# Batches 0 and 1 as a pair with seven block products for eight, in a fused attention and MLP kernel

## The chip, the cores and the metric

The kernel runs on one core of a Trainium2 chip. The metric is device time in microseconds, the median over executions of the same program. A core has five engines that work side by side, each through its own instructions in order: TensorE (PE in the profile, with its weight loads as PEld), VectorE (DVE), ScalarE (ACT), GpSimd (POOL) and SyncE (SP, which here only issues DMAs). Semaphores order them among each other.

## The reference

Attention with 16 query heads on 4 key and value heads, then an MLP block on its output:

```python
def _attn_ref(q, k, v):               # q (8,16,384,64), k and v (8,4,384,64)
    ...
    scores = scale * np.matmul(q, k.transpose(0, 1, 3, 2))
    ...                               # softmax
    return np.matmul(attn, v)

def _moe_ref(x, alpha1, beta1, w_tok, alpha2, beta2, w_ch1, w_ch2, lam):
    a1 = alpha1 * x + beta1           # x (8,384,1024): the heads side by side
    tok = np.einsum('ts,bsd->btd', w_tok, a1)
    u = x + lam * tok
    a2 = alpha2 * u + beta2
    ch = np.maximum(a2 @ w_ch1, 0.0) @ w_ch2      # 1024 -> 4096 -> 1024
    return u + lam * ch
```

Most of the arithmetic is in the two large products, with W1 (`w_ch1`) and W2 (`w_ch2`).

## The kernel before

Matmuls take bf16 operands and sum in fp32 PSUM banks. One batch is 384 tokens. Weights come from HBM in fp32 and are cast by DMAs that POOL issues (`load_w1`: 512 KB in bf16 per chunk of 256 columns, into a ring of six slots; `load_w2`, quarters and rows of W2).

**Batches 0 and 1** are worked singly. `side(0)` is batch 0's attention, written out as a list of steps: `k_transpose` and `q_transpose` (turned on PE), `scores(i)` (18 pieces; each ends with an exp on ACT into one of six places in `hT`), `av(p)` for a pair of heads (product with v, then reciprocal and scaling on DVE), `a1(p)` (times alpha1 on DVE), `tok(p)` (token product with the transposed `w_tok`, which `wtok_transpose` turns; the beta row comes as one more matmul of `R` and `H`; then u on DVE), and `a2_transpose(p)`, which for batch 0 turns u on PE (L357) and scales it with alpha2 on ACT. `main(b)` then makes all of the first product (`h`: 256 matmuls of 384 columns, L532, for batch 0 partly L223) and all of the second (`ch`: 192 of 512 columns, L570) for the one batch. Batch 1's attention stands among main(0)'s matmuls, that of batches 2 and 3 among main(1)'s. The table `plan` says at which step of which stage each piece of work is recorded.

**The later batches** go in pairs, `pair(i)`: with two batches as two block rows, each product is made of seven block products instead of eight. In the first product (`X`, `Y`, `Z`, L723) a slice g covers two column tiles e of each half of W1: seven products o of four matmuls for each e. The left sides come from `opb(k)`, made by `sums_a` on DVE; the right ones are W1 blocks or their differences (`sum_w1`, four on DVE per slice). In the second product (`C`, L789) seven products of three row tiles and 16 matmuls each run over `hid`, with W2's blocks and their combinations, which `sum_w2` made once on DVE and put into seven scratch tensors `w2s` in HBM, from where `fetch` reads them for every pair. The next two batches' attentions are recorded among the second product's matmuls, their k and q turned by DMA (`flip_k`, `flip_q`, issued by SP), a2 made on DVE and turned by DMA (`a2_transpose`) or for a few pieces on PE (`turn`). `spill` writes u to the output; the product's result is added to it by an accumulating DMA (`store`), scaled by lam on DVE (`scaled`).

The order on each engine is the order of recording in the source (`tc.manual_schedule`): nothing is moved by a scheduler. The alpha2, beta1 and lam rows reach all partitions by way of `load_row_set` (four copies of half a row by an SP DMA) and `to_all` (a shuffle on DVE). POOL issues its DMAs on eight semaphores in turn, so that one waits for the eighth before it.

Of the kernel before, what the change touches and what calls it, by code (L numbers as in the profile page):

```python
# [12 lines left out]
def kernel(  # L13
# [21 lines left out]
    nc = tc.nc  # L35
# [10 lines left out]
    G = Hq // Hkv  # L46
# [9 lines left out]
    NPL = 2  # L56
# [14 lines left out]
    threes, pairs = [], {}  # L71
# [5 lines left out]
    w2 = arena.rearrange("p (t h d) -> p t h d", t=NH, h=2)  # L77
    hid = arena.rearrange("p (t e) -> p t e", t=NH)[:, :, :5 * S].rearrange("p t (k s) -> p t k s", k=5)
    w1 = const.tile([P, RING, NDT, CW * P], bf, tag="w1", name="w1")
# [5 lines left out]
    BE = NDT // 2 * S  # L85
    ops = const.tile([P, 7 * BE], bf, tag="ops", name="ops")
    a2Ts = [ops[:, :NDT * (S + 16)].rearrange("p (a s) -> p a s", a=NDT),
            ops[:, 5 * BE:].rearrange("p (a s) -> p a s", a=NDT)]

    def opb(k):  # L90
        return ops[:, k * BE:(k + 1) * BE].rearrange("p (a s) -> p a s", a=NDT // 2)
# [26 lines left out]
    def row(nt):  # L118
        return nt % NH, nt // NH
# [21 lines left out]
    def load_k(b, hs=(0, 2)):  # L141
        if b > 1:
            k_tile(b)
            for a in range(2):
                nc.gpsimd.dma_start(out=k2s[b][:, :, a], in_=by_head(k[b]))
            return
        for h in hs:
            ks[b, h // 2] = t = hTf[:, 7680 + 384 * h:8448 + 384 * h].bitcast(f32).rearrange(
                "p (h st d) -> p h st d", h=2, st=NST)
            nc.sync.dma_start(out=t, in_=by_head(k[b, h:h + 2]))  # L150

    def place_k(b, i, hs=(0, 1)):
        if b not in k2s:
            k_tile(b)
        copies = [nc.gpsimd.tensor_copy] * 2
        if b == 1 or b == 0 == i:
            copies = (nc.vector.tensor_copy, nc.vector.tensor_copy if i else nc.scalar.copy)
        lo, hi = hs[0], hs[-1] + 1
        for a in range(2):
            copies[a](out=k2s[b][:, 2 * i + lo:2 * i + hi, a], in_=ks[b, i][:, lo:hi])  # L160
# [26 lines left out]
    def load_w2(dw, r, h):  # L187
        cs = slice(dw * 512, (dw + 1) * 512)
        nc.gpsimd.dma_start(out=w2[:, 4 * r:4 * r + 4, h, cs], in_=w2src[:, h * NH + 4 * r:h * NH + 4 * r + 4, cs])

# [5 lines left out]
    def three():  # L196
        if pairs:
# [11 lines left out]

    def evac(eng):  # L210
        return nc.scalar.copy if eng == "ACT" else nc.vector.tensor_copy


    early = {}
    FIRST = (0, 1, NH, NH + 1)
# [844 lines left out]
```

## Time and profile before

| what | us |
| --- | --- |
| median of 3 timed runs (739.28 to 741.14) | 739.38 |
| span of the profiled execution, first to last instruction | 737.7 |
| PE busy in it | 731.3 |
| DVE busy | 515.4 |
| ACT busy | 325.2 |
| POOL busy, its DMA issues with it | 164.0 |
| start of the first product's unbroken part (L532) | 36.3 |
| first matmul of the second product of batch 0 (L570) | 74.9 |
| first matmul of the pair's first product (L723) | 242.1 |

The profiled execution has no time of its own beside its span; the median of the timed ones is 1.65 us above the span. Busy times count each instruction from its start to its end, and pipelined matmuls overlap, so that the distance from one start to the next is the price of one. Each timeline line gives start, length, engine, source line, operation, output and input, shapes and count; a line of the stretches gives span, and for each engine busy time and instructions, then the granted TensorE clock, the DMA share and GB/s. The page's GB/s row has 40 equal slices of the span.

### The profile page before, as it was taken

What the parts mean: (1) busy time and instruction counts of PE and PEld (TensorE: products, weight loads), DVE (VectorE), ACT (ScalarE), POOL (GpSimd) and SP (SyncE); (2) the same over time, 40 slices, a digit from 0 to 9 for tenths busy, and PEclk for the clock granted to TensorE, in tenths of its full rate; (3) what the DMA queues carried; (4) which work ended last, traced back from release to release, by engine and by line L of the source; (5) the groups of instructions that cost most, each with busy time, mean ns of one, the idle gap of its engine ahead of it and who ended that gap; (6) DMA issues with size and microseconds to landing.
All of it is one profiled execution on the core that took longest, in us unless ns stands there. A gap on an engine that the chain in (4) does not pass through costs nothing.

```text
span 737.7 us, 14512 instructions
## 1 busy us (share of the span) xinstructions
PE 731.3 (99%) x5769; PEld 418.9 (57%) x5769; DVE 515.4 (70%) x993; ACT 325.2 (44%) x469; POOL 164.0 (22%) x211
## 2 busy tenths in 40 slices
PE   8999999999999999999999999999999999999998
PEld 5866555566555566655555566555555566654444
DVE  7773366457587889749777987847968988762354
ACT  7632431455332566653334366664343266660000
POOL 9434221420000232211012244020002222000011
PEclk9999999999999999999999999999999999999999
DMA  9999999999999999999979999998989999937965
GB/s 187 194 201 200 207 216 174 176 187 208 217 271 257 179 221 212 260 269 201 296 186 219 181 145 192 207 246 199 269 242 152 223 136 143 173 115 262 288 189 103
DMA packets 218017, 151.32 MB, mean 205 GB/s; under 512 B 88660, under 2 KB 197060, under 8 KB 217948
## 3 DMA queue, kind: packets, MB, share of 16 engines
q0 software_dynamic: 120304, 64.60, 67.0%
q1 hardware_dynamic: 96956, 85.33, 42.7%
q8 instruction: 45, 0.74, 0.4%
q10 hardware_dynamic: 688, 0.46, 0.2%
q14 instruction: 24, 0.20, 0.1%
HBM read 154.84 MB, written 38.27 MB: 262 GB/s over the span
## 4 chain that ended last, share of the span: by engine, by line
PE 93%; DVE 3%; DMA 3%; SPq 1%; issue 0%; ACT 0%; DVEq 0%
PE C L789 30%; PE X L723 17%; PE h L532 10%; PE ch L570 9%; PE Y L723 8%; PE sc L279 4%; PE Z L723 4%; PE sc L315 4%; PE sc L340 3%; DMA ops<-a 2%; PE h L223 1%; DMA hT<-in_moe_lam_dram 1%; PE tok L340 1%; SPq L176 0%; PE av L315 0%; DVE xr L323 0%
## 5 line engine op out<-in xcount | busy, mean ns | idle before, releaser
L288 ACT ACTIVATE es<-sc 128x1024 bf16<-128x1024 f32 x126 | 121.4, 1023 | 155.9 <-PE sc L279 144.8
L789 PE MATMUL C<-w,arena 128*128 128x512 bf16 (+2 forms) x744 | 168.3, 372 | 0.0
L789 PEld LDWEIGHTS <-arena 128*128 128x128 bf16 x1040 | 94.8, 98 | 100.5 <-issue 5.1
L728 ACT ACTIVATE hT<-X,bias 128x384 f32<-128x384 f32 x144 | 83.7, 582 | 61.8 <-PE X L723 54.8
L723 PEld LDWEIGHTS <-w 128*128 128x128 bf16 x768 | 75.1, 98 | 50.1 <-issue 0.2
L517 POOL DMA_DIRECT2D out_dram<-hT x33 | 28.8, 871 | 283.5 <-DVE hT L688 106.1
L570 PE MATMUL ch<-arena,hT 128*128 128x512 bf16 x384 | 90.8, 379 | 0.0
L185 POOL DMA_DIRECT2D w<-in_moe_w_ch_dram x68 | 62.8, 965 | 98.2 <-PE X L723 34.2
L532 PE MATMUL h<-ops,w 128*128 128x384 bf16 (+1 forms) x480 | 83.3, 327 | 0.3
L723 PEld LDWEIGHTS <-pad 128*128 128x128 bf16 x576 | 56.4, 98 | 37.2
L723 PE MATMUL X<-ops,w 128*128 128x384 bf16 x384 | 70.2, 326 | 0.0
L723 PE MATMUL X<-ops,pad 128*128 128x384 bf16 x384 | 70.2, 326 | 0.0
L789 PE MATMUL C<-pad,arena 128*128 128x512 bf16 (+2 forms) x296 | 70.2, 373 | 0.0
L532 PEld LDWEIGHTS <-w 128*128 128x128 bf16 x480 | 45.4, 98 | 29.8 <-issue 2.1
L570 PEld LDWEIGHTS <-hT 128*128 128x128 bf16 x384 | 34.7, 98 | 36.8 <-issue 2.5
L347 DVE TENSOR_TENSOR xr<-sc,xr 128x384 f32<-128x384 f32 x56 | 31.0, 553 | 24.3 <-PE sc L340 24.3
L315 PEld LDWEIGHTS <-es 128*128 128x128 bf16 x1008 | 38.3, 97 | 12.4
L340 PEld LDWEIGHTS <-wtokT 128*128 128x128 bf16 x576 | 37.5, 98 | 11.8 <-DVE a L330 0.8
L279 PE MATMUL sc<-qT,kT 64*128 64x384 bf16 (+2 forms) x576 | 41.8, 271 | 0.7 <-DVE xr L323 0.3
L320 DVE RECIPROCAL rinv<-sc 128x6 f32<-128x6 f32 x56 | 10.8, 192 | 44.3 <-PE sc L315 44.1
L315 PE MATMUL sc<-v,es 128*128 128x65 bf16 x1008 | 39.9, 193 | 0.0
L723 PE MATMUL Z<-ops,w 128*128 128x384 bf16 x192 | 39.0, 326 | 0.0
(138 smaller groups left out, 910.3 us busy)
## 6 DMA issues: line engine op xcount, KB each, us to landing
w<-in_moe_w_ch_dram POOLq DMA_DIRECT2D x68, 512.0 KB, 10.7
w<-w2s SPq DMA_DIRECT2D x60, 512.0 KB, 4.6
pad<-w2s SPq DMA_DIRECT2D x24, 512.0 KB, 7.2
out_dram<-xr SPq DMA_DIRECT2D x56, 192.0 KB, 6.1
out_dram<-hT POOLq DMA_DIRECT2D x33, 256.0 KB, 6.0
arena<-in_moe_w_ch_dram POOLq DMA_DIRECT2D x16, 512.0 KB, 20.0
w2s<-arena SPq DMA_DIRECT2D x28, 256.0 KB, 4.9
q_raw<-in_q_dram POOLq DMA_DIRECT2D x28, 192.0 KB, 10.6
```

The lines of the kernel that those rows point to most:

```text
L185: nc.gpsimd.dma_start(out=w1[:, w1_slots[c]], in_=w1src[:, :, c * CW * P:(c + 1) * CW * P])
L279: nc.tensor.matmul(out=sc[:, hh, k % 4:k % 4 + n], lhsT=kT[r, 2 * p // G, BLK[hh][sk], :], rhs=qT[r, p, st:st + n, :], start=True, stop=True)
L288: nc.scalar.activation(out=e, in_=sc, func=EXP, scale=scale_qk)
L315: nc.tensor.matmul(out=av[:, hh, sq, :], lhsT=ess[k // 4][:, m % 2, k % 4, :], rhs=vb[:, sk, hk, :], start=(sk == 0), stop=(sk == NST - 1))
L340: nc.tensor.matmul(out=ps[:, tt, :], lhsT=wtokT[:, st, tt * P:(tt + 1) * P], rhs=a1s[p][:, st, :], start=(st == 0), stop=(st == NST - 1 an ...
L347: nc.vector.tensor_tensor(out=u, in0=ps, in1=u, op=ADD)
L517: nc.gpsimd.dma_start(out=at, in_=o, accum_op=ADD)
L532: nc.tensor.matmul(out=ps[:, :n], lhsT=w1[:, w1_slots[c], dt, j * P:(j + 1) * P], rhs=a2T[:, dt, :n], start=(dt == 0), stop=(dt == NDT - 1))
L570: nc.tensor.matmul(out=ps, lhsT=hT[:, nt, ms * P:(ms + 1) * P], rhs=w2[:, row(nt)[0], row(nt)[1], cs], start=(i == 0), stop=(i == NNT - 1))
L723: nc.tensor.matmul(out=ps, lhsT=tb[g, o][:, dt, e * P:(e + 1) * P], rhs=opb(LEFT1[o])[:, dt], start=(o in (1, 2, 7) and dt == 0), stop=(dt ...
L728: nc.scalar.activation(out=snap[o, e], in_=ps, func=IDENT, bias=hi if o == 5 else lo)
L789: nc.tensor.matmul(out=x, lhsT=hid[:, t, LEFT2[o], ms * P:(ms + 1) * P], rhs=rhs[:, t % 4 * 512 + c0:t % 4 * 512 + c1], start=((not last o ...
```

## The change

Batches 0 and 1 become the first pair, `pair(0)`, in place of the two `main` stages, and the other three follow as `pair(1)` to `pair(3)`. Both attentions stand ahead of the product: 36 steps of `scores`, 18 for each batch, with the other work in a table (`A` is batch 0, `C` batch 1), and the last pieces of batch 1 between the product's first six groups. Batch 1's k and q are turned by DMA; both batches use the first batch's form of a1 and tok (alpha1 product alone, beta by the row matmul). a2 is made on POOL for batches 0 to 3, except the last three pieces of batches 1 and 3 (DVE), and turned by DMA, those three by `turn`. alpha2's rows are loaded early, into the arena beside `k2s[1]`.

This pair uses another set of left sides (`FIRST1`, `sums_first`, `diff_first`), 385 columns in four of the seven products for the bias column, and other sums of the hidden blocks (`sums_first_hid`). `second_product` reads W2's quarters as they were loaded, in the order 2, 1, 5, 3, 6, 7, 4: `sum_w2` writes each difference over a quarter in place, `keep_w2` copies each operand to `w2s` for the later pairs, and the quarter "21" is read back from there for the last. The product with lam in `scaled` is on POOL in this pair.

```diff
-        first = b == 0
+        first = b < 2
...
-            a2s[p] = next_a2() if b > NPL + 1 else sb.tile([P, NST, P], bf, tag="a2", name="a2", bufs=2)
-            nc.vector.tensor_tensor(out=a2s[p], in0=u, in1=bc(al2, p), op=MUL)
+            a2s[p] = next_a2()
+            eng = nc.gpsimd if b < 4 and not (b % 2 and by_pe(p)) else nc.vector
+            eng.tensor_tensor(out=a2s[p], in0=u, in1=bc(al2, p), op=MUL)
...
+    def sums_first(j, n=1):
+        js = slice(j, j + n)
+        tt(out=opb(2)[:, js], in0=opb(0)[:, js], in1=opb(1)[:, js], op=ADD)
+        tt(out=opb(0)[:, js], in0=opb(2)[:, js], in1=opb(3)[:, js], op=SUB)
+
+    def diff_first(j, n=1):
+        js = slice(j, j + n)
+        tt(out=opb(5)[:, js], in0=opb(3)[:, js], in1=opb(0)[:, js], op=SUB)
...
+    def keep_w2(o, c):
+        nc.sync.dma_start(out=w2s[4 * PLACE2[o] + c], in_=raw[{1: "11", 2: "21", 3: "22", 5: "12", 6: "12", 7: "11", 4: "again"}[o], c][1])
+
+    def sum_w2(o, c):
+        at = lambda name: raw[name, c][1]
+        to, x, y = {5: ("12", "12", "11"), 6: ("12", "22", "12"), 7: ("11", "12", "11"), 4: ("again", "again", "12")}[o]
+        tt(out=at(to), in0=at(x), in1=at(y), op=SUB)
+        keep_w2(o, c)
...
+SEQ0 = tuple((o, e) for o in (1, 7, 2, 6, 5, 3, 4) for e in range(2))
+FIRST1 = {**LEFT1, 6: 0, 7: 5}
+FIRST2 = {1: 0, 2: 3, 3: 3, 4: 1, 5: 2, 6: 0, 7: 2}
...
+    def second_product(acc, later, flush, scaled):
...
+        for o in (2, 1, 5, 3, 6, 7, 4):
+            for ms in range(NST):
+                x = acc.tile([P, 512], f32, tag="acc", name="C", bufs=2)
+                for t in range(NH):
+                    slot, rhs = raw[names[o], t // 4]
+                    nc.tensor.matmul(out=x, lhsT=lead_hid[:, t, FIRST2[o], ms * P:(ms + 1) * P],
+                                     rhs=rhs[:, t % 4 * 512:(t % 4 + 1) * 512], start=(t == 0), stop=(t == NH - 1),
...
-        place_k(0, 0, (0,))
-        load_w1(order1[0])
-        load_w1(order1[1])
-        place_k(0, 1)
+        place_k(0, (0,))
+        load_q(1)
+        for a in range(2):
+            nc.gpsimd.dma_start(out=k2s[1][:, :, a], in_=by_head(k[1]))
+        place_k(1)
         scale_rows(1, nc.gpsimd)
         split(1, 2, None, nc.gpsimd)
-        for c in order1[2:RING]:
+        for i in range(2):
+            nc.gpsimd.memset(rows4[i], 0.0)
+            load_row_set(2, i, i)
+        load_v(1)
+        for c in order1[:RING]:
             load_w1(c)
...
+        for c in range(4):
+            put(0, 0, 40 + 8 * c, load_w2, "11", c)
+            put(0, 1, 1 + c, keep_w2, 2, c)
+            put(0, 1, 5 + c, keep_w2, 1, c)
+            put(0, 1, 12 + 2 * c, sum_w2, 5, c)
+            put(0, 1, 28 + c, keep_w2, 3, c)
+            put(0, 1, 24 + c, sums_first_hid, 2, c)
+            put(0, 1, 29 + c, sums_first_hid, 4, c)
+            put(0, 1, 36 + 2 * c, sum_w2, 6, c)
+            put(0, 1, 37 + 2 * c, sums_first_hid, 3, c)
+            put(0, 1, 45 + 2 * c, sum_w2, 7, c)
+            put(0, 1, 52 + 2 * c, sum_w2, 4, c)
...
+              9: [(A.wtok_transpose, 0, "av"), (A.wtok_transpose, 1, "tp"), (to_all, 2, 0, 0)],
+              10: [(A.wtok_transpose, 2, "av"), (A.q_transpose, 6, 2, "mm"), (fill_h, 0)], 11: [(A.av, 3), (A.rows_r, "tp")],
+              12: [(A.spread, upper, "av"), (A.a1, 2), (to_all, 2, 1, 1)], 13: [(A.tok, 0), (A.av, 4), (A.a1, 3), (flip_q, 1, 4, 2)],
...
+        for i in range(36):
+            (C if i >= 18 else A).scores(i % 18)
+            for f, *a in at.get(i, []):
+                f(*a)
+        for f, *a in ((product, 2), (C.av, 7), (C.a1, 7), (C.tok, 6), (C.turn, 5, "tp"), (diff_first, 2, 2), (sums_first, 0, 1), (product, 2),
+                      (C.tok, 7), (C.turn, 6, "av"), (sums_first, 1, 1), (product, 2), (C.turn, 7, "tp"), (sums_first, 2, 2)):
+            f(*a)
```

## The prediction

> **What bounds the kernel now.** I read the page first, for which engine is full:
>
> ```profile
> PE 731.3 (99%) x5769; PEld 418.9 (57%) x5769; DVE 515.4 (70%) x993; ACT 325.2 (44%) x469; POOL 164.0 (22%) x211
> PE 93%; DVE 3%; DMA 3%; SPq 1%; issue 0%; ACT 0%; DVEq 0%
> ```
>
> TensorE is busy all through, and the chain that ended last runs over it for 93% of the span. So a matmul taken out is worth its spacing, as long as nothing else becomes late. The spacing I read from the chain in order of time, in stretches without a gap:
>
> ```profile
> 59.66 2.61 PE h L532 x16
> 85.59 2.59 PE ch L570 x12
> ```
>
> A matmul of 384 columns costs 2.61/16 = 0.163 us, one of 512 columns 2.59/12 = 0.216 us. Then the stretch that the change rebuilds, the lead-in. The table by stretches and the timelines of PE and DVE show:
>
> ```profile
> 6.00:27.00 21.00, 20.27 (x326) 14.71 (x326) 18.60 (x46) 19.31 (x24) 15.51 (x24) 1.00 1.44 197
> 14.84 0.52 PE L369 MATMUL tp<-ident,arena 128*128 128x128 bf16 x6
> 20.05 0.54 DVE L334 TENSOR_TENSOR hT<-pad,vecs 128x384 bf16<-128x384 f32 x1
> 20.52 0.54 DVE L347 TENSOR_TENSOR pad<-tok,pad 128x384 f32<-128x384 f32 x1
> ```
>
> From 6 to 27 us PE (20.3 of 21), DVE (18.6) and ACT (19.3) are all nearly full, and the DMA rings move 197 GB/s: there is no engine to give work to. One 384-wide DVE product or sum follows the next after 0.47 us. Elsewhere DVE and ACT have slack.
>
> **What the change takes from TensorE.** First product: 512 matmuls become 448, 64 x 0.163 = 10.5 us less. Second product: 384 become 336, 48 x 0.216 = 10.4 less. Eight times three fp32 transposes of u (L357; the trace has them 0.33 us per three) go, 2.6. Batch 1's k and q are turned by the DMA, 36 transposes of 0.055 fewer; six more turns of a2 and 24 more row matmuls in tok (0.055 each) come: net -0.3. Together 23.9 us. If all stayed covered, the span of 737.7 would be 713.8. The timed executions have a median of 739.38, 1.65 us above that span; I add the same.
>
> **What it moves into the lead-in.** Attention of batch 1 stood among batch 0's first-layer matmuls and its second product; now both attentions stand ahead of the product. By PE alone: batch 0's part ended at 36.27 with 32 h matmuls (5.2) and the u transposes (2.6) in it, so 28.5 without. Batch 1 adds 18 scores of 0.33, 8 av of 0.60, 8 tok of 0.67 and 3 turns of 0.17, 16.6 in all, and six groups of products (24 x 0.163 = 3.9) stand in the lead-in's end. A dense PE would be there at 49.0.
>
> It will not be dense, for two reasons. The first is a new wait. The alpha2 rows now come early, as two row loads into the arena, and in the changed program the first wtok transpose (14.84 above) waits for both to land; SP issues them only when both k loads of batch 1 have landed. Ahead of these stand the four q loads of batch 1. In the trace a 192 KB cast load lands about 1.0 us after the one before it (q_raw: issued 17.6 to 19.8, landed 13.6 to 14.4 us later), and the load of q heads 12 to 15 lands at 6.4 + 7.1 = 13.5. Six more loads: 19.5. The second row load leaves half a us later. Its landing is bounded below by nothing measured, by 3.2 for a 192 KB load into empty rings, and above by the 4.5 us seen for row loads under traffic, which I work out from these:
>
> ```profile
> 33.94 1.19 SPq L927 DMA_DIRECT2D rows<-in_moe_lam_dram  x2
> SPq L927 <- DMA rows<-in_moe_lam_dram: 2.7, 1, 2.7
> ```
>
> (issued at 33.94; SP's third issue ends at 35.7, then the 2.7 of waiting for this load: 38.4). No W1 load stands in the rings by then, so I take 3.0: PE goes on at 23.0, bounds 21 to 24.5. Behind the waiting PE stand scores, so ACT runs dry, and DVE has nothing from PE either.
>
> The second is DVE, which then sets the pace. It still has, at the spacings of the trace: thirteen pairs of reciprocal and scaling at 0.69 (five of batch 0, eight of batch 1), 14 a1 and 16 tok sums at 0.47, 23.1 us; copies, fills and the two new shuffles (0.72 each), 5.5; four W1 differences of 0.68, 2.7; the seven-product sums of the activations, 3.6; three a2, 1.4. Sum 36.3. PE has 34 and ACT 26 exps x 0.94 = 24. In 16.95 to 25.77 DVE worked 8.4 of 8.8 us, so 3 to 5% comes on top: 37.5. With half a us for the first transposes the lead-in ends at 23.0 + 0.5 + 37.5 = 61.0, **12.0 us after a dense PE**.
>
> After eight idle microseconds PE may come back slow: the nine warm-up matmuls at the start take 3.06 us where nine cost 1.5 later. That is 1.5 us more of PE work, which the 3.5 us between 34 and 37.5 covers; uncovered it costs 1.5. The Trainium skill (TensorE: Matmul & The Clock Gate, "Part 1: The HAM clock gate") says that the array falls to half clock after an idle window of about 3.4 us and needs as long to come back. By that rule the sum would be the same; no row here shows it after a gap, since before has none.
>
> **The rest.** The a2 products of batches 0 to 3 go to POOL behind the W1 loads: POOL issues these from 20 to 26 (the six chunks then land 2.65 us apart, by about 40; DVE reads the first two at about 44), and the first a2 is due at 28. Thirteen products fit into the 33 us left: a cast grows from 0.28 us at 128 elements to 0.55 at 384, a product starts at 0.45 and grows by as much or twice as much, so 0.72 to 0.99 (an estimate). Their turns stand on SP at 1.29 + 0.55 us per piece, 16 pieces in 30 us: it fits, and the flips that batch 1 needs next stand between them with more than 4 us to spare. Hand-over from the lead-in's PSUM banks to the pair's, and pairs of X groups waiting for ACT's 0.58 copy in the first slice: bounds 0 to 2, I take 1. First product otherwise as in the other pairs: DVE 7.4 and ACT 6.6 of 9.1 us per slice. In the second product DVE has 16 sums of 1.33 (two of the 0.68 rows), 12 of 0.95, 21 evacuations of 0.61 and two attentions of 17: with the small ones about 87 of 105 us, which PE hides. W2's second quarters are issued from 128 on, 3 us ahead of that product, and at 512 KB per 2.65 us (197 GB/s) the four are there by 139; DVE reads them 15 to 23 us into the product, so that half the bandwidth would do. Bounds 0 to 13 (a rival below); I take 2.
>
> Sum: 713.8 + 12.0 + 1 + 2 + 1.65 = **730.5 us**, 1.2% faster.
>
> **Rivals.**
> *The row loads don't bind.* If they land before 15, DVE still sets the pace: 15.4 + 37.5 = 52.9, 3.9 after a dense PE: 713.8 + 3.9 + 1 + 1.65 = 720. For it: none of the bytes is large. Against: six loads stand ahead. 0.13.
>
> *The second product becomes DMA's.* It now has to move what stood in three stages: 28 stores of W2's operands (512 KB each, 14.7 MB), the quarters "12" and "22" as they load (4.2), one quarter back (2.1), spills 3.1, output adds 3.1, W1 heads 2.1: 29.3 MB in 105 us, 279 GB/s. The page has this:
>
> ```profile
> GB/s 187 194 201 200 207 216 174 176 187 208 217 271 257 179 221 212 260 269 201 296 186 219 181 145 192 207 246 199 269 242 152 223 136 143 173 115 262 288 189 103
> ```
>
> Single slices reach 296, but the three busiest neighbours (217, 271, 257) average 248. At that rate it takes 118 us, 13 more instead of my 2: 741.5, slower by 0.3%, and more if DVE stands in order behind a late quarter. It decides below about 260 GB/s. Against it: stores may lag into the next product. 0.20, with 0.12 of it beyond 741.6, as its upper end is long.
>
> *DVE and POOL in each other's way.* POOL's a2 reads two SBUF operands beside DVE ops that do too. In the trace POOL's scalar product took 0.78 beside such a DVE product (12.36) and 0.61 otherwise, while that DVE product kept its 0.56: POOL pays, 13 x 0.2, hidden. If DVE paid instead 0.7 us for each of 13, the lead-in would be 9 longer: 739.5. A chance of 0.10. The Trainium skill (SBUF — State Buffer, section "SBUF: two separate sides") says that the two share a port pair, locked for a whole instruction by whoever starts first, the other blocked fully; by that rule DVE would pay in about half of the cases, 735 us. The trace agrees in that one of the two lost time, but it was 0.17 us and not a whole instruction.
>
> **How the numbers follow.** Forecast 0.57, range of its own 725 to 736 (the wait 21 to 24.5, the two takings from zero to 2 and 5). This kernel's measurement can tell about 0.3%, 2.2 us, from no change: faster is below 737.2, slower above 741.6. Faster: 0.56 of the forecast, 0.13 without the wait, 0.02 of the DMA case, 0.02 of the POOL case: 0.73. Same: 0.01, 0.06 and 0.04 of forecast, DMA and POOL: 0.11. Slower: 0.12 of the DMA case, 0.04 of the POOL case: 0.16. The range of 720 to 742 leaves out the DMA case's upper end (0.11) and what lies under the case without the wait (0.07).
>
> **What would show it.** Step by step: PE MATMULs 5626; a gap of about 8 us on PE ending near 23 us with a DMA landing of the arena's alpha2 rows as its releaser; the first slice's first group of product 6 near 61; the first product's 424 remaining matmuls dense, ending near 131; the second product about 107 us without a DVE wait for W2 over 2 us. I am wrong if PE doesn't stop at the wtok transposes, if the lead-in after it takes much under 37 us, or if DVE's W2 differences wait for `arena<-` or `w<-` loads of W2.

## The result: 6.6% slower, and the profile after

The changed kernel takes 789.21 us (median of 4 runs, 783.16 to 792.25) against 740.1 for the kernel before (4 runs, 739.28 to 741.14). The ratio is 1.0655, with a 95% interval of 1.061 to 1.0699. The forecast of 730.5 and the range up to 742 were wrong. The profiled execution has a span of 787.6 us. Its page, in the lines that answer to those shown of before (busy times, the chain's shares, the granted clock and the bytes in 40 slices):

```profile
PE 724.0 (92%) x5568; PEld 409.3 (52%) x5626; DVE 566.1 (72%) x1033; ACT 351.4 (45%) x515; POOL 217.8 (28%) x255
PE 61%; DVE 2%; DMA 2%; issue 1%; DVEq 0%
PEclk9889599999999999999999999999999999999999
GB/s 159 157 179 137 67 122 189 211 291 194 248 273 262 257 144 182 183 198 237 189 269 222 171 225 156 195 221 209 198 293 183 230 160 132 152 118 265 274 190 113
```

The program has the 5626 matmuls that were forecast (x5626 weight loads). But PE is busy for 92% of a longer span, and its chain share fell from 93% to 61%. The fifth clock digit is 5: half speed around 80 to 98 us (0.50 over 81 to 98). PE's timeline shows the places, with the wait and its releaser in brackets:

```profile
22.30 0.80 PE L324 MATMUL tp<-ident,arena 128*128 128x128 bf16 x6 [6.79 <-DMA arena<-in_moe_alpha_dram]
53.86 1.04 PE L243 MATMUL sc<-qT,kT 64*128 64x384 bf16 x8 [5.34 <-DMA kT<-arena]
79.70 0.80 PE L659 MATMUL X<-ops,pad 128*128 128x384 bf16 x2 [2.78 <-DVE ops L434]
87.25 1.44 PE L659 MATMUL X<-ops,w 128*128 128x385 bf16 x4 [0.62 <-ACT hT L671]
96.34 2.73 PE L659 MATMUL X<-ops,w 128*128 128x385 bf16 x8 [0.80 <-DVE arena L685]
```

The first gap was forecast, the second was not. After both the granted clock was 0.50 for a while (22 to 24 us and 53.8 to 56.3). At 87 us a group of four matmuls takes 1.44 us from its first start to its last end, where 0.81 is usual (the group at 66.96). The table by stretches (span, busy time of PE, PEld, DVE, ACT and POOL, granted clock, DMA share, GB/s) has the first slice with its clock of 0.59, slices 1 to 7, the second product, and the same stage of the next pair:

```profile
75.00:100.00 25.00, 16.32 (x57) 6.69 (x56) 11.90 (x24) 6.40 (x14) 4.73 (x7) 0.59 0.51 67
...
96.30:164.80 68.50, 66.55 (x393) 38.80 (x394) 49.56 (x102) 40.96 (x85) 24.19 (x31) 0.98 1.22 182
164.80:292.00 127.20, 104.03 (x905) 55.19 (x921) 97.97 (x146) 42.02 (x49) 48.14 (x44) 0.97 1.11 240
364.80:465.20 100.40, 99.11 (x906) 54.67 (x921) 76.87 (x146) 38.15 (x43) 11.95 (x14) 1.00 0.95 222
```

The second product takes 127.2 us, with the same number of matmuls as the next pair's, which takes 100.4. What follows it is unchanged: 787.6 - 292.0 = 495.6 us, and before 737.7 - 242.1 = 495.6. So all of the loss lies ahead of 292 us. Against the forecast of 728.85 us of span (730.5 less 1.65) it is 58.7 us too long, by place (the parts make 58.5, the rest is rounding):

| place | forecast | measured | too long by |
| --- | --- | --- | --- |
| lead-in, to product 6 of the first slice | 61.0 | 76.1 | 15.1 |
| rest of the first slice (8 groups) | 6.2 | 20.2 | 14.0 |
| slices 1 to 7 | 63.9 | 68.5 | 4.6 |
| second product (the sum leaves it 100.4, and adds 2) | 102.4 | 127.2 | 24.8 |

### The profile page after: what moved, and what is told of

Read it like the earlier page. It is cut to its first block, busy times and chain, and to the rows that moved or that the text cites. A ratio compares the mean times of both kernels' runs of the same rounds, so it can differ in the third digit from the quotient of the medians.

```text
span 787.6 us, 14312 instructions
## 1 busy us (share of the span) xinstructions
PE 724.0 (92%) x5568; PEld 409.3 (52%) x5626; DVE 566.1 (72%) x1033; ACT 351.4 (45%) x515; POOL 217.8 (28%) x255
## 4 chain that ended last, share of the span: by engine, by line
PE 61%; DVE 2%; DMA 2%; issue 1%; DVEq 0%
PE C L749 26%; PE X L659 16%; PE Y L659 8%; PE Z L659 4%; PE sc L243 2%; PE sc L278 2%; DMA out_dram<-xr 2%; PE sc L304 2%; PE C L552 1%; DVE a1f L291 0%; DVE xr L286 0%; DVE xr L311 0%; DVE arena L621 0%; PE sc L377 0%; DVE hT L786 0%
## 5 line engine op out<-in xcount | busy, mean ns | idle before, releaser
L749 PEld LDWEIGHTS <-arena 128*128 128x128 bf16 x1040 | 94.7, 98 | 100.6 <-issue 5.1
L659 PEld LDWEIGHTS <-w 128*128 128x128 bf16 x1024 | 100.7, 99 | 75.5 <-issue 10.5
L659 PE MATMUL X<-ops,pad 128*128 128x384 bf16 (+1 forms) x512 | 96.6, 331 | 4.7 <-DVE ops L434 2.9
L659 PE MATMUL X<-ops,w 128*128 128x384 bf16 (+1 forms) x512 | 96.6, 332 | 3.0 <-ACT hT L671 1.2
L659 PE MATMUL Y<-ops,w 128*128 128x384 bf16 x256 | 52.2, 326 | 2.9 <-DVE ops L438 1.9
L659 PE MATMUL Z<-ops,w 128*128 128x384 bf16 (+1 forms) x256 | 52.0, 326 | 0.0
L659 PE MATMUL Y<-ops,pad 128*128 128x384 bf16 x256 | 48.2, 332 | 2.5 <-DVE arena L683 1.1
L552 PEld LDWEIGHTS <-arena 128*128 128x128 bf16 x336 | 30.6, 99 | 32.2 <-issue 4.3
L252 ACT ACTIVATE hT<-sc 128x1024 bf16<-128x1024 f32 x36 | 35.3, 1025 | 23.0 <-PE sc L243 22.7
L304 PE MATMUL sc<-a,wtokT 128*128 128x128 bf16 x432 | 32.6, 221 | 13.3 <-DVE a L293 13.3
L483 DVE TENSOR_TENSOR pad<-w,pad 128x1024 bf16<-128x1024 bf16 x64 | 43.6, 682 | 0.0
L552 PE MATMUL C<-w,arena 128*128 128x512 bf16 x161 | 41.3, 388 | 0.5 <-issue 0.2
```

The costliest lines, as they stand in the source:

```text
L252: nc.scalar.activation(out=e, in_=sc, func=EXP, scale=scale_qk)
L304: nc.tensor.matmul(out=ps[:, tt, :], lhsT=wtokT[:, st, tt * P:(tt + 1) * P], rhs=a1s[p][:, st, :], start=(st == 0), stop=(st == NST - 1 an ...
L483: tt(out=t, in0=x, in1=y, op=SUB)
L552: nc.tensor.matmul(out=x, lhsT=lead_hid[:, t, FIRST2[o], ms * P:(ms + 1) * P], rhs=rhs[:, t % 4 * 512:(t % 4 + 1) * 512], start=(t == 0), ...
L659: nc.tensor.matmul(out=ps[:, :n], lhsT=tb[g, o][:, dt, e * P:(e + 1) * P], rhs=opb(left[o], n)[:, dt], start=(o in (1, 2, 7) and dt == 0), ...
L749: nc.tensor.matmul(out=x, lhsT=hid[:, t, LEFT2[o], ms * P:(ms + 1) * P], rhs=rhs[:, t % 4 * 512 + c0:t % 4 * 512 + c1], start=((not last o ...
```

## The experiments

All are variants of the changed kernel. The table gives the median time, the ratio to the kernel before with its interval, the span of the profiled execution, and in it the start and length of the first pair's second product (from PE's timeline) and the traffic in it (from the table by stretches). Medians scatter by some us; stages are compared by the profiles. They scatter too: in nine kernels with one and the same lead-in, product 6 starts at 76.1 to 79.4, and in five with one and the same second product it takes 117.7 to 119.8. So from one profile each, 2 to 3 us are not told apart.

| kernel | us | ratio (95%) | span | second product from | takes | GB/s |
| --- | --- | --- | --- | --- | --- | --- |
| changed kernel | 789.21 | 1.0655 (1.0610 to 1.0699) | 787.6 | 164.8 | 127.2 | 240 |
| first_tiles | 775.64 | 1.0467 (1.0433 to 1.0501) | 779.6 | 156.8 | 126.2 | 242 |
| rows_apart | 786.31 | 1.0634 (1.0575 to 1.0694) | 786.5 | 163.8 | 127.1 | 240 |
| dve_products | 793.14 | 1.0719 (1.0696 to 1.0743) | 790.0 | 165.5 | 127.0 | 241 |
| xr_five | 781.15 | 1.0551 (1.0531 to 1.0571) | 780.1 | 166.4 | 117.9 | 259 |
| rows_k_pe | 788.89 | 1.0665 (1.0624 to 1.0706) | 787.1 | 164.8 | 126.7 | 241 |
| no_sums | 784.32 | 1.0604 (1.0587 to 1.0621) | 781.8 | 165.1 | 119.5 | 256 |
| keep_twice | 800.55 | 1.0819 (1.0795 to 1.0843) | 798.6 | 166.2 | 136.1 | 267 |
| all_four | 770.38 | 1.0424 (1.0399 to 1.0449) | 768.9 | 154.0 | 117.7 | 257 |
| lead_turns_pe | 775.33 | 1.0475 (1.0442 to 1.0508) | 777.3 | 161.5 | 119.7 | 255 |
| second_turns_pe | 773.78 | 1.0446 (1.0413 to 1.0479) | 774.4 | 154.6 | 123.6 | 237 |
| spills_pool | 769.73 | 1.0399 (1.0368 to 1.0429) | 767.6 | 153.0 | 119.0 | 256 |
| keeps_early | 779.49 | 1.0531 (1.0500 to 1.0562) | 781.1 | 159.2 | 120.1 | 250 |
| lead_all_pe | 765.46 | 1.0338 (1.0316 to 1.0360) | 763.2 | 149.1 | 118.1 | 258 |
| no_stores | 776.26 | 1.0481 (1.0455 to 1.0507) | 777.8 | 168.5 | 112.4 | 251 |
| no_sums_no_stores | 771.81 | 1.0425 (1.0401 to 1.0449) | 769.0 | 164.9 | 108.3 | 261 |
| no_sums_spills_pool | 785.41 | 1.0623 (1.0579 to 1.0668) | 789.3 | 167.8 | 112.9 | 263 |
| bytes_on_act | 808.53 | 1.0943 (1.0899 to 1.0986) | 806.5 | 166.1 | 144.3 | 255 |
| lead_av_first | 765.46 | 1.0355 (1.0317 to 1.0394) | 762.6 | 147.4 | 119.8 | 256 |

### The first slice

**first_tiles**

```diff
-                if e == 0:
-                    leads[name] = bank([P, 2, 512], "sc", name)
-                return leads[name][:, e]
+                if name == "X":
+                    leads[e] = bank([P, 2, 512], "sc", name)
+                return leads[e][:, int(name == "Y")]
```

> The changed kernel, with X and Y of the first slice laid out otherwise: one PSUM tile for each e (X in its first bank, Y in its second) in place of one tile for X of both e and one for Y of both e. Theory A (false order): in the changed kernel every group of four matmuls there takes 1.44 us and then waits 0.6 us for ACT's copy of the group before, since both stand in one tile; two tiles in turn take the wait away, PE fills, and its clock comes back. The stretch from 76 to 96 us shrinks by 8 to 15 us, the span from 787.6 to 773 to 780, and groups take 0.65 us. Theory B (the clock alone: the array is slow on account of the long gaps before, whatever the tiles): the groups keep 1.44 us, only the 0.6 us waits go, a gain of 3 us or less. Theory C (what is lost lies in the second product alone): the gain is given back there, 0 to 2 us in all.

Measured, in first_tiles' timeline of PE and its table by stretches:

```profile
81.27 3.83 PE L659 MATMUL X<-ops,pad 128*128 128x384 bf16 x14 [2.78 <-DVE ops L434]
85.06 1.47 PE L659 MATMUL X<-ops,w 128*128 128x385 bf16 x8
```

```profile
75.00:100.00 25.00, 20.18 (x123) 11.37 (x121) 16.64 (x35) 10.92 (x23) 7.29 (x11) 0.93 0.69 100
```

Eight matmuls take 1.47 us instead of four in 1.44, and the granted clock over 75 to 100 us is 0.93 (0.59 in the changed kernel). From product 6 to slice 1 it is 12.1 us (77.7 to 89.8) for 20.2, and the span falls by 8.0. Theory A holds. That the clock stayed slow was a result of the false order: PE stopped 0.57 to 0.62 us for ACT's copy behind every 1.44 us of work, since two independent groups shared one tile. A first slow stretch is in both kernels, behind the wait of 2.8 us: in first_tiles the 14 matmuls after it take 3.83 us, some 1.4 more than at full clock, and then the clock is back. What else is left of the stage is that wait, for the sums of the last pieces, and 0.91 and 0.84 us of waits for DVE.

### The lead-in

**rows_apart** and, on top of it, **rows_k_pe**

```diff
-        rows4 = [arena[:, 13824 + 1024 * i:14848 + 1024 * i].bitcast(f32) for i in range(2)]
+        rows4 = [part(4 + i).bitcast(f32) for i in range(2)]
...
-              17: [(A.av, 6), (A.a1, 6), (flip_k, 1, 2, 2), (flip_q, 1, 6, 2)],
+              17: [(A.av, 6), (A.a1, 6), (C.k_transpose, 2, 2, "tp"), (flip_q, 1, 6, 2)],
```

> The changed kernel, with the two alpha2 row tiles put into `pad`, which is unused that early, in place of `arena`, so that neither the row loads nor the wtok transposes stand behind the loads of batch 1's k. Theory A (the wait on the row loads costs what it shows): PE's gap of 6.8 us before 22.3 us goes, and the lead-in ends 5 to 7 us earlier: span 781 to 783. Theory B (the gap is swallowed: the second gap, which ends at 53.9 us with the turn of batch 1's k, is set by SP's DMA turns and the weight loads and stays where it is): the second gap grows by as much, and the gain is 0 to 2 us.

> The kernel of rows_apart, in which also the second half of batch 1's k is turned on PE (C.k_transpose into a tp bank, copied by DVE) in place of SP's turn flip_k(1, 2, 2), which stands behind four turns of a2. rows_apart alone gave 1.1 us of span of the 6.8 that it freed. Theory A (two waits in series, and the second one swallowed the first): now the gap of 6.4 us before 52.9 us goes too, the lead-in ends 6 to 9 us earlier than in rows_apart, span 777 to 781. Theory B (the gap is the W1 loads' or POOL's: something else is late at the same place): another wait takes its place there and the gain over rows_apart is under 3 us.

In rows_apart the gap of 6.8 us before 22.3 is gone, and 1.1 us of span are gained, no more than the scatter: Theory B's gain, but not quite its way. The second gap grew by only 1.0 (to 6.4); PE now waits 2.1 us at 20.6 for DVE and 3.0 at 33.4 for the turn of k's first half. In rows_k_pe the second gap is gone too, and nothing is gained (787.1): Theory B again, something else is late at the same place. DVE's waits from 15 to 85 us in rows_k_pe say what came instead:

```profile
DVE arena L311 <- PE tok L308: 8.5, 9, 2.2
DVE ops L438 <- DMA ops<-obuf: 4.6, 1, 4.6
```

DVE stands 4.6 us for turned a2 of batch 1. So I looked at SP, which issues these turns. Its timeline in the changed kernel, while the W1 loads travel and after them (start, length of the issue):

```profile
39.01 2.90 SPq L317 DMA_TRANSPOSE ops<-obuf  x1
43.64 2.37 SPq L317 DMA_TRANSPOSE ops<-obuf  x1
46.74 3.29 SPq L160 DMA_TRANSPOSE kT<-arena  x1
...
61.91 1.25 SPq L317 DMA_TRANSPOSE ops<-obuf  x1
```

POOL, which makes a2, waits for a place in the ring of five `obuf` places until such a turn has emptied one:

```profile
47.71 1.00 POOL L314 TENSOR_TENSOR obuf<-arena,vecs 128x384 bf16<-128x384 f32 x1 [5.57 <-DMA ops<-obuf]
```

**all_four** puts first_tiles, rows_apart, the PE turn of k and xr_five (below) together. **lead_turns_pe** then takes five turns of batch 1 from SP and POOL, **lead_all_pe** all 13 of both batches from SP:

```diff
-            return b % 2 and p >= NP - 3
+            return b < 2 or b % 2 and p >= NP - 3
...
+        for m, us in ((A, (16, 17, 18, 19, 21, 23, 24, 25)), (C, (27, 29, 31, 33, 35))):
+            for p, u in enumerate(us):
+                at.setdefault(u, []).append((m.turn, p, "tp" if p % 2 else "av"))
```

> first_tiles, rows_apart, the PE turn of k and xr_five together. If the losses lie in separate places and add (theory A): 13.6 of first_tiles, 8 of xr_five and 8 to 11 of the two waits of the lead-in off 789.2, time 755 to 760, still 15 to 20 us above the kernel before, which is what the second product (about 123 against 105) and the lead-in's DVE pace keep. If they cover each other (theory B): 768 or more.

> The kernel of all_four (span 768.9), in which the first five pieces of batch 1's a2, too, are made on DVE and turned on PE, in place of POOL's product and SP's turn. In rows_k_pe and all_four the freed gaps came back as other waits, and DVE then stood 4.5 us for the turned pieces 0 and 1 (ops<-obuf at L438); from 26 to 68 us SP issued 13 turns and 16 spills in one row, a turn taking 1.25 to 4.6 us for the predicted 1.29. Theory A (SP's row of turns paces the lead-in): without five of its turns the 4.5 us go and POOL no longer waits for a free place of the a2 ring; the lead-in ends 5 to 8 us earlier, span 761 to 764. Theory B (the lead-in is paced by the chain of latencies PE, DVE, PE in each piece): gain 0 to 2 us, or a loss of 1 to 3, as DVE has five products of 0.56 more.

> The kernel of all_four (span 768.9), in which all 16 pieces of a2 of batches 0 and 1 are turned on PE, three to six steps after their token product, and copied by ACT; a2 itself stays where it was (POOL, the last three of batch 1 DVE). In lead_turns_pe, which took only batch 1's pieces from SP, DVE stood 7.1 us for a place in the a2 ring, that is for an earlier piece of batch 0 that SP's DMA turn had not brought over yet. Theory A (the DMA turns under the weight loads' traffic pace the lead-in, by the ring of five and by SP's row): with none left, the ring is free after ACT's copy, the waits of 1.5 to 4.5 us between 45 and 66 us go, and the first slice's product 6 starts 6 to 12 us earlier than at 79; span 757 to 763. Theory B (POOL's 1.0 to 1.25 us a2 and the in-order latency of each piece pace it): less than 3 us, with PE 2.2 us fuller.

all_four: the time, 770.38, is in Theory B's range, but that the gains cover each other is not shown. The spans of its parts (first_tiles, xr_five, rows_k_pe) fall by 8.0, 7.5 and 0.5 us, and its own by 18.7; the medians by 13.6, 8.1 and 0.3, and its own by 18.8. What failed was the 8 to 11 us that I gave the lead-in's waits, of which product 6 got 0.7 (75.5 for 76.1), or some 2 by the means (75.4 in four kernels with all_four's lead-in, 77.7 in nine with the old one). lead_turns_pe was 8.4 us slower, against both theories, and its DVE timeline gave the reason:

```profile
50.80 0.56 DVE L314 TENSOR_TENSOR obuf<-arena,vecs 128x384 bf16<-128x384 f32 x1 [7.11 <-DMA ops<-obuf]
```

The ring of five a2 places was still full of batch 0's pieces, which SP's turns had not brought over; now DVE stood for them in place of POOL. In lead_all_pe, with no DMA turn of a2 left, product 6 starts at 69.1 (76.1 in the changed kernel) and the span is 763.2, 5.7 below all_four: Theory A, at the small end of its range. **lead_av_first** changes the order that is left:

```diff
-              24: [(C.tok, 0), (C.av, 1), (C.a1, 1)], 26: [(C.tok, 1), (C.av, 2), (C.a1, 2), (sum_w1, 0, 5)], 27: [(sum_w1, 0, 7)],
+              24: [(C.av, 1), (C.a1, 1), (C.tok, 0)], 26: [(C.av, 2), (C.a1, 2), (C.tok, 1), (sum_w1, 0, 5)], 27: [(sum_w1, 0, 7)],
...
```

> The kernel of lead_all_pe (span 763.2), in which for batch 1 the token product of piece p is recorded behind the product with v of piece p + 1 in place of ahead of it. In lead_all_pe each piece there takes 3.05 us or more, and PE waits 0.55 to 1.4 us in each for DVE's a1 of that piece. Theory A (the latency from PE to DVE and back paces batch 1's half of the lead-in): the waits at tok nearly go, the spacing of pieces falls to 2.3 to 2.7 us, and the first product begins 3 to 5 us earlier: span 758 to 761. Theory B (DVE or ACT has no more to give there): less than 1.5 us.

The waits of PE at tok for a1 (0.55 to 1.4 us each) nearly go, and product 6 starts 2.2 us earlier, at 66.9: half of what Theory A expected, and within the scatter. The second product then is 1.7 us longer, and the time is the same, 765.46. So of the 15.1 us above the forecast at product 6, 7.0 went with the two gaps and the DMA turns together, where the gaps alone gave 0.7 to 2, and 2.2 with the change of order; the other 5.9 were not taken apart.

### The second product

**dve_products**

```diff
-            eng = nc.gpsimd if b < 4 and not (b % 2 and by_pe(p)) else nc.vector
+            eng = nc.gpsimd if b < 2 and not (b % 2 and by_pe(p)) else nc.vector
...
-                (nc.gpsimd if lead else nc.vector).tensor_tensor(out=t, in0=t, in1=lam_t[:, dw * 512:(dw + 1) * 512], op=MUL)
+                nc.vector.tensor_tensor(out=t, in0=t, in1=lam_t[:, dw * 512:(dw + 1) * 512], op=MUL)
```

> The changed kernel, with the alpha2 product of batches 2 and 3 and the lam product of the first pair's `scaled` on DVE in place of POOL; the lead-in is left as it is. DVE gets 13 products of 0.56 and 12 of 0.69 us more, 15.5 us. Theory A (DVE and POOL in each other's way): DVE's ops of two SBUF operands fall back from 0.78 (L293) and 1.22 us (L540) to the 0.56 and 0.95 that they take in the later pairs, which gives 11.6 us back; POOL's 1.47 us products leave the way from u to the turned a2, and the second product shrinks from about 131 to 118 to 126 us: span 775 to 783. Theory B (the second product is held by DMA traffic): its 236 GB/s stay, and the span changes by less than 3 us. Theory C (DVE is full there, and more work makes it later): 1 to 5 us slower.

Groups of DVE in that stage (busy, mean ns), first the changed kernel, then dve_products:

```profile
L540 DVE TENSOR_TENSOR arena<-arena 128x1536 bf16<-128x1536 bf16 x12 | 14.3, 1216 | 0.0
L293 DVE TENSOR_TENSOR a<-a1f,vecs 128x384 bf16<-128x384 f32 x16 | 12.5, 779 | 0.6
```

```profile
L540 DVE TENSOR_TENSOR arena<-arena 128x1536 bf16<-128x1536 bf16 x12 | 11.1, 950 | 0.0
L293 DVE TENSOR_TENSOR a<-a1f,vecs 128x384 bf16<-128x384 f32 x16 | 8.9, 558 | 0.6
```

DVE does pay for POOL's products, and the stretch is gone when POOL has none. But the stage takes 127.0 us for 127.2: Theory A's mechanism is there and its price is not. The time is 4 us above the changed kernel's and the span 2.4; Theories B and C both allow that.

**xr_five**

```diff
-                xr[p] = sb.tile([P, NST, P], f32, tag="xr", name="xr", bufs=4)
+                xr[p] = sb.tile([P, NST, P], f32, tag="xr", name="xr", bufs=5)
```

(obuf is cut to 960 columns to make the room.)

> The changed kernel, with five buffers for `xr` in place of four, so that DVE's scaling (L286) finds a free one while spills still travel. Theory A (the buffers bind): of DVE's 11.8 us of waiting for the spills of xr in the second product at most a third is left, and the span falls by 3 to 8 us, to 780 to 785. Theory B (the traffic or the order on SP binds): the same spills are waited for one piece later or SP's turns come later in their place, and the span changes by less than 2 us.

DVE's waits for spills there, in the changed kernel and in xr_five (us in total, times, longest):

```profile
DVE xr L286 <- DMA out_dram<-xr: 11.8, 4, 6.0
```

```profile
DVE xr L286 <- DMA out_dram<-xr: 1.3, 1, 1.3
```

They became 1.3 us, and the stage 9.3 us shorter: Theory A. In the 117.9 us it moves as many bytes, 0.259 x 117.9 = 30.5 MB, as in 127.2 (0.240 x 127.2 = 30.5).

**no_sums** (the two `tt(...)` lines of `sum_w2` and `sums_first_hid` taken out) and **keep_twice** (in `keep_w2`, for o in 1, 2 and 3, a second `nc.sync.dma_start` to a DRAM tensor of its own), both on xr_five

> The kernel of xr_five, which leaves out the first pair's 16 differences of W2's quarters and 12 differences of hidden blocks in the second product (28 DVE ops, about 35 us of DVE busy time there; the stores of W2's operands stay). Theory A (DVE is overfull in the steps where these sums stand, and PE waits in order for attention's products behind them): PE's 11 us of waits for DVE (a L293, xr) nearly go and the second product, about 123 us in xr_five, takes 107 to 112: span 764 to 770. Theory B (DMA traffic sets that stage's pace, 29 MB or more in it): the traffic is the same and the span changes by less than 3 us. Theory C (only POOL's stretching of DVE): with DVE light, the stretch of 0.56 to 0.7 us stays and some 3 to 6 us are gained.

> The kernel of xr_five, in which 12 of the 28 stores of W2's operands (those of the products 2, 1 and 3) are made twice, the second time to DRAM tensors that nobody reads: 6.3 MB more in the second product, 21% of the 29.3 MB of the prediction. Theory A (the traffic hides, DVE's order sets the pace): at most 4 us slower than xr_five, span 780 to 784. Theory B (bandwidth sets the pace at the 236 GB/s that this stage shows): 6.3 MB cost 20 to 27 us, span above 798.

This overturned my theory that DVE's sums hold the stage. Without 28 of DVE's 144 ops the stage takes 119.5 us, 1.6 more (within the scatter). DVE was busy for 64 us of it, and waited longer for its spills:

```profile
DVE xr L286 <- DMA out_dram<-xr: 18.8, 5, 6.7
```

With 6.3 MB more it takes 136.1, and DVE's W2 differences wait for their loads:

```profile
DVE w L474 <- DMA w<-in_moe_w_ch_dram: 13.8, 2, 12.5
DVE pad L474 <- DMA pad<-w2s: 7.2, 1, 7.2
```

Theory B in both, though the 18.2 us are less than the 20 to 27 it expected: 18.2 / 6.3 = 2.9 us per MB. The added stores also stand in SP's row of issues, which the next runs try.

**second_turns_pe**, **spills_pool** and **keeps_early**, on all_four, try whether it is SP's row of issues:

```diff
-            return b % 2 and p >= NP - 3
+            return b in (2, 3) or b % 2 and p >= NP - 3
-                put((36, 39, 41)[p - NP + 3], turn, p)
+                put((11, 18, 20, 25, 30, 36, 39, 41)[p], turn, p)
... spills_pool
-            nc.sync.dma_start(out=by_tok(out[b])[:, :, cols(p)], in_=x_of(p))
+            (nc.gpsimd if b in (2, 3) else nc.sync).dma_start(out=by_tok(out[b])[:, :, cols(p)], in_=x_of(p))
... keeps_early
-            put(0, 1, 5 + c, keep_w2, 1, c)
+            put(0, 0, 56 + 8 * c, keep_w2, 1, c)
```

> The kernel of all_four, in which all 16 pieces of a2 of batches 2 and 3 are turned on PE (13 of them by SP so far; a2 itself stays on POOL). From 200 to 260 us SP issues nearly without a pause in all runs with that product (turns of a2 at 2 to 3 us, of k at 10), and no_sums has shown that DVE's sums are not what holds the stage. PE gets 13 x 0.17 = 2.2 us more, ACT 13 x 0.48. Theory A (SP's row, each DMA turn in it long, holds the second product): SP is relieved of some 25 us, PE's waits of 13.6 us for DVE shrink to a third, span 755 to 762. Theory B (bytes, at 250 to 280 GB/s): 13 turns are 1.3 MB, 5 us at the most, less the 2.2 of PE: span 766 to 769. Theory C (the way POOL, PE, ACT is later than the old one, or PSUM places are short): slower than 770.

> The kernel of all_four, in which POOL issues the 16 spills of batches 2 and 3, each right behind its a2 product, in place of SP. The same bytes. Theory A (SP's row): SP loses 16 issues of 0.55 to 2 us and, above all, spills don't stand behind turns and stores; xr comes free earlier, span 760 to 766. Theory B (bytes): within 2 us of 768.9. Theory C: POOL's row, with W1's and W2's loads in it, becomes later by 16 x 0.9 us, span above 771.

> The kernel of all_four, in which the four stores of W2's quarter 11 (2.1 MB, no sum in it) stand in the first product, where the rings move 130 to 217 GB/s, in place of the first steps of the second. keep_twice has shown that 6.3 MB more in that stage cost 19 us. Theory A (bytes): 2.1 MB less give a third of that, 5 to 7 us, span 762 to 764. Theory B (it is SP's row around 200 to 260 us, where these four don't stand): gain under 2 us.

No a2 turn of these batches on SP: 5.9 us longer (Theory C), with PE waiting 9.6 us in the stage for POOL's a2. Spills on POOL: 1.3 longer in the stage and 1.3 less in the span (B). 2.1 MB moved ahead: the second product starts 5.2 us later, takes 2.4 more, and the next pair's first product 79.0 instead of 74.3, a loss that neither theory expected. The stage hardly became lighter by it, 30.1 MB for 30.2, so it says little of bytes. What is moved costs in the stage where it goes.

**no_stores** (`if not lead:` ahead of `store` in `scaled`), **no_sums_no_stores** and **no_sums_spills_pool**, on xr_five:

> The kernel of xr_five (second product 117.9 us; the later pairs' takes 100.4), which leaves out the first pair's twelve accumulating stores (3.1 MB), so that batches 0 and 1 stay without the MLP's part. With the next two it makes a square: sums in or out, stores in or out. Theory A (bytes hold the stage): 8 to 12 us less, 106 to 110. Theory B (DVE's sums hold it): under 3 us less. Theory C (both stand at their limit, either alone gives nothing): under 4 us less here, as no_sums alone gave nothing, and much in no_sums_no_stores.

> The kernel of xr_five without the 28 sums of no_sums and without the 12 stores of no_stores. Theory A (bytes): as no_stores. Theory B (sums): as no_sums, about 119. Theory C (two limits close to each other): 103 to 109 in the second product, more than the two single gains together; span 765 to 771.

> The kernel of no_sums (second product 119.5 us), with the spills of batches 2 and 3 issued by POOL in place of SP. In no_sums DVE waits 18.8 us for xr to be spilled, with SP inside stores of W2's operands or turns of 3 to 10 us just before each of those spills. Theory A (SP's row, where a spill stands behind long issues, takes the place of DVE's sums as the limit): the waits for xr fall under 5 us and the second product to 104 to 110. Theory B (bytes: spills land late wherever they are issued): 117 to 120 as before.

The square, in us of the second product: 117.9 with both, 119.5 without the sums, 112.4 without the stores, 108.3 without either. The stores are worth 5.5 us with the sums (between the theories of no_stores) and 11.2 without them; the sums nothing with the stores and 4.1 without them. Theory C's size came out, but not its form, since one limit leads: the stores, with DVE close behind. Whether by their bytes, POOL's twelve issues of them or the tiles that they hold is not told apart. In no_sums_spills_pool the stage falls to 112.9 (between the theories), and the next pair's first product takes 84.7 us for 73.7 in no_sums, as DVE stands 9.4 us there for the last turned pieces of a2; nothing is gained in all.

**bytes_on_act** puts the 6.3 MB on ACT's queue:

```diff
+        def copy_more(j):
+            nc.scalar.dma_start(out=more[j], in_=raw["11", j % 4][1])
+
+        for j in range(12):
+            put(0, 1, 2 + 2 * j, copy_more, j)
```

> The kernel of xr_five (second product 117.9 us at 259 GB/s), with twelve more stores of 512 KB in the second product's steps 2 to 24, issued by ACT, of W2's quarter 11, which has long been loaded, to DRAM tensors that nobody reads: the 6.3 MB of keep_twice, but SP's row and its waits stay as they are. Theory A (bytes: eight variants moved 250 to 267 GB/s in this stage, whatever was taken out or put in, so 6.3 MB cost 24 us at that rate): second product and the next first product together 14 to 25 us longer, as in keep_twice (19). Theory B (SP's row is the limit, and keep_twice lost its 19 us by twelve more issues in it): less than 7 us longer.

The stage takes 144.3 us, 26.4 more: more than Theory A expected, and not Theory B as it was put. But the run is not as clean as I meant it to be. ACT's waits there have a new entry:

```profile
ACT hT L568 <- DMA out_dram<-xr: 11.9, 1, 11.9
ACT es L253 <- DMA out_dram<-xr: 10.4, 1, 10.4
```

Nothing that ACT computes or stores there needs a spill of xr. In the trace's issues of bytes_on_act the DMAs of SP and ACT take eight semaphores in turn, as POOL's do, and each issue waits until the DMA that had its semaphore before has landed; so the twelve more stores can hold these up too, here as in keep_twice, and ACT's exps and PE behind them. The stage by kernel (span, engines, clock, DMA share, GB/s) for xr_five, no_sums_no_stores, keep_twice, bytes_on_act and second_turns_pe:

```profile
166.40:284.30 117.90, 106.71 (x923) 56.33 (x921) 95.78 (x144) 41.95 (x49) 47.27 (x44) 0.96 1.16 259
```

```profile
164.90:273.20 108.30, 102.47 (x922) 55.07 (x921) 60.71 (x116) 41.65 (x49) 34.36 (x35) 0.98 1.14 261
```

```profile
166.20:302.30 136.10, 108.05 (x906) 57.25 (x921) 95.28 (x144) 42.22 (x49) 48.05 (x45) 0.91 1.13 267
```

```profile
166.10:310.40 144.30, 108.88 (x905) 57.68 (x921) 92.94 (x144) 41.71 (x49) 48.85 (x44) 0.88 1.08 255
```

```profile
154.60:278.20 123.60, 108.68 (x945) 58.15 (x961) 94.22 (x144) 48.06 (x62) 48.43 (x44) 0.96 1.03 237
```

In the first four, with 28.3, 30.5, 36.3 and 36.8 MB, the stage takes 108, 118, 136 and 144 us: the time rises with the traffic, at 255 to 267 GB/s. But bytes alone don't set it. The 30.5 MB took 127.2 us with four places for xr and 117.9 with five; no_stores and no_sums_no_stores moved 28.2 MB each, in 112.4 and 108.3; and second_turns_pe has 29.3 MB, fewer than xr_five, and takes longer. So it is shown that the places for xr held the stage for 9.3 us, and that DVE's sums do not hold it while the stores are there. That its DMAs hold it fits all of this; whether by bytes, by the eight semaphores, or by the mix of casting loads, turns, accumulating stores and 512 KB stores was not told apart. 20 us of keep_twice (260 to 280) moved 346 GB/s, so the rate is no hard ceiling.

No variant beats the kernel before; the best two have 765.46 us, 3.4 and 3.6% above it by their ratios. In lead_av_first 25.0 of the 58.7 us are back. What stays above the forecast is 5.9 us in the lead-in, 6.3 in the rest of the first slice, 4.2 in slices 1 to 7 and 17.4 in the second product.

## Why the prediction was wrong, point by point

Three terms of the sum failed: the lead-in's 12.0 us after a dense PE, the 1 of the first slice and, the largest, the 2 of the second product. The other terms held or cost little.

**PE's saving was right.** The 5626 matmuls are there, and the stages behind 292 us are unchanged. A dense PE would be at the second product at 118.1 (49.0 + 69.1); with the 100.4 us that a later pair's takes and the unchanged 495.6 this makes 714.1, against the 713.8 of the sum. The check "about 107 us" for that product contradicted the sum, which left 102.4.

**The first wait was right, its worth wasn't.** It ended at 22.3 (forecast 23.0), 6.8 us long, behind the row loads. But taking it away gave 1.1 us. The rival "the row loads don't bind" gave 720, 10.5 us less, by the same error as the next step (and left out the second product's 2 us: with them it is 722.4).

**The lead-in's pace failed at the step "Their turns stand on SP at 1.29 + 0.55 us per piece ... it fits ... with more than 4 us to spare".** I took the price of a turn from a quiet stretch. Beside W1's loads, from 32 to 46 us, one took 1.2 to 2.9 us (k's 3.3) in the changed kernel, and the five places of the a2 ring handed that on to whoever made a2. The step that DVE "then sets the pace" failed with it: DVE was busy for only 14.2 of the 21 us from 54 to 75. What sets the pace of the 5.9 us that are left stays open.

**The first slice's 1 us (0 to 2) was 15.** I had named the wait for ACT's copy, but counted it once and not for every group, and not that PE's clock would fall with it. The clock term looked at one gap of eight us, and behind that gap the clock was indeed 0.50 (22 to 24 us); but short gaps in a chain did the harm. The Trainium skill (TensorE: Matmul & The Clock Gate, section "A second HAM failure mode: psum-queue depth-cycling") tells of micro-idles between matmul groups that make the clock swing between half and full. The trace agrees in that short gaps hold the clock down, though here it did not swing: it was 0.50 from 81 to 98, at gaps of 0.57 to 0.91 us. With two such gaps left, first_tiles has 0.93 over 75 to 100.

**Slices 1 to 7 were not dense, 4.6 us more.** The sum had nothing for that. The first eight matmuls, still at a slow clock, cost 1.2 us more (96.34 to 98.87), two waits of Y for DVE 1.0, and a pause of 0.3 in each slice ahead of Y, whose releaser the profile doesn't name, about 2.

**The second product's 2 us (0 to 13) was 24.8.** The changed kernel took 127.2 us for it, and the rival "the second product becomes DMA's" gave 118. It pointed the right way, to DMA waits, but by bytes over a rate alone, and that does not give 127.2: the changed kernel moved 30.5 MB at 240 GB/s. That xr_five shows 117.9 is luck in part, at 259 GB/s and 30.5 MB for 248 and 29.3. The rate was misread too: the three busiest neighbours of that row are 269, 201 and 296, 255 on average, which gives 115 us. And the sign that it named came out small: DVE waited 2.0 and 1.0 us for W2's loads in the changed kernel, and 11.8 for spills. I set the rival aside with "stores may lag into the next product"; in keeps_early and no_sums_spills_pool what was moved or lagged was paid in the other stage. It left out the buffers: four places for xr made spills under traffic a wait of DVE, 9.3 us more. What sets the other 15.5 us is open, as said above.

**DVE and POOL: one row was made a rule.** I saw that POOL pays, in one row of a 128-column POOL product. In the second product DVE paid, 0.22 us a piece at L293 and 0.27 at L540, and POOL's a2 took 1.47 us on average for 1.0 at best. In the lead-in, where the rival stood, DVE's a1 products (L298) took 0.62 for 0.55 before, a us in all, and POOL's thirteen a2 1.09 each for the 0.72 to 0.99 of the estimate. The Trainium skill (SBUF — State Buffer, section "SBUF: two separate sides") has the pair locked for a whole instruction, the other side blocked. The trace agrees in part: one op of L293 took 2.00 us, 1.44 more than its 0.56, beside a POOL product of 1.01, which is not all of it. In the second product's time it cost nothing that could be seen (127.2 us with POOL's products, 127.0 without).

## What to carry to other kernels

When stages are merged, add up the bytes of the merged stage, divide by the rate that a stretch of the same length has shown, and let that number stand beside the engines' work as a forecast, not as a rival; then ask which buffers wait for those transfers, for they came on top here. Take the price of a DMA turn from a stretch with the same traffic, and follow its ring of buffers to the engine that fills it. Two independent groups in one tile were one chain here: count a wait per group, and a slower TensorE on top.

## What the runs showed of the hardware that I had not expected

TensorE ran at a granted clock of 0.59 for 25 us (75 to 100), and of 0.50 from 81 to 98, though it was never idle for longer than 2.8 us there. A DMA turn of 96 KB held SP's queue for 1.25 us in quiet and 1.2 to 2.9 beside loads; one of k held it for 9.7 us in the second product (202.0, changed kernel). DMAs that SP and ACT issued shared eight semaphores, so that ACT stood 11.9 and 10.4 us for spills that SP had issued (bytes_on_act).
